# Two transformer layers on one core: running the first attention group inside the neighbouring stages, repeating score matmuls, and keeping the MLP partial sums in SBUF

## The chip, the cores and the metric

The kernel runs on one core of one Trainium2 chip. The metric is the device time of a whole execution in microseconds (us). Executions of the same kernel spread by about 1% here (before: 1991 to 2008 us in its first four runs), so small differences are judged by ratios from interleaved rounds on one chip, with a 95% interval.

The engines are called by their profile names: PE (matmul), PEld (weight load), ACT (activation), DVE (vector), POOL, SP. *Clock* is always the granted TensorE clock of the profile, as a share of full speed. In the profile lines, `S` is a score tile, `P` its exponentials, `tp` a score chunk that DVE copied out, `misc` a PSUM tile of the fill work, `ustg` a staging buffer, `uacc` the partial sums in DRAM and `y` the second MLP product. *PV* is the product of the exponentials with V.

## The reference

```python
x = A_x                                    # 1 x 2048 x 640, bf16
x = x + attention(layernorm(x), wqkv, wo)  # 32 heads of 20
x = x + token_mlp(layernorm(x), w1, b1, w2, b2)   # mixes the 2048 tokens, 1536 hidden, tanh-gelu
x = x + attention(layernorm(x), wqkv, wo)  # same weights again
x = x + token_mlp(layernorm(x), w1, b1, w2, b2)
```

The attention has 4 query blocks of 512, 8 groups of 4 heads and 16 key tiles of 128. One *chunk* is the 128 x 512 score block of one head and one key tile. A layer has 2048 chunks, and each needs an exponential of all its elements.

## The kernel before

A layer of attention is one loop over score tiles of three chunks. PE makes the scores of tile t+1, ACT turns tile t into exponentials, DVE takes one chunk in some of the tiles (five instructions on DVE that build the exponential from bits), and PE multiplies by V. What else PE has to do (projections, output projection, first MLP product) waits in a *fill queue* and is put into the gaps that a small cost model sees.

```python
emit_S(0, 1)
for t in range(NTILES):
    cur_t[0] = t
    if t + 1 < NTILES:
        emit_S(t + 1, 1)            # scores: 3 matmuls of 32 x 128 rows, computed once
    pv_ready(force_t=t - CFG["PT_BUFS"])
    ...
    emit_exp(t)                     # ACT: 3 chunks, or 2 while DVE takes one
    dve_run(clk["act"] - 0.4)
    pv_ready()
    emit_fills(clk["act"], misc_alloc)
```

The token MLP sums over tokens, so its first product can begin with the first query blocks. Before, each of query blocks 0 to 2 makes a partial sum of four token tiles. Every partial sum is copied by DVE into one of two staging buffers, and POOL sends it to DRAM. The second and third partial sums are added there by accumulating DMAs.

```python
ustg = p1.enter_context(tc.tile_pool(name=f"ustg{layer}", bufs=2))
...
def evac(t, ft=ft, c0=c0, c1=c1, w=w):
    stg = ustg.tile([128, 512], F32, name="ustg")
    dve_cost(0.1 + w / 960.0)
    nc.vector.tensor_copy(out=stg[:, 0:w], in_=t[:, 0:w])
    dst = uacc_l[ft * 128:(ft + 1) * 128, c0:c1]
    if p == 0:
        nc.gpsimd.dma_start(out=dst, in_=stg[:, 0:w])
    else:
        nc.gpsimd.dma_start(out=dst, in_=stg[:, 0:w], accum_op=ALU.add)
```

Around the attentions lie four other stages: a prologue (load, LayerNorm, transposes, V, first K and Q), a tail with the first MLP product, a middle stage (second MLP product of layer 0 fused with LayerNorm, transposes, V, first K and Q of layer 1), and at the end the second MLP product of layer 1. No exponential runs in these.

The softmax here doesn't subtract the row's maximum and nothing guards it: scores larger than these inputs give would overflow.

## Time and profile before

1998.11 us median of 4 runs; the profiled execution has a span of 1997.3 us. I cut it into stages with the first and last exponential of each layer and the first matmul that writes `y` (the second MLP product), all read from the timeline:

| stage | from | to | us | bound by |
|---|---|---|---|---|
| prologue | 0 | 49.1 | 49.1 | input DMA, then PE |
| attention 0 | 49.1 | 921.1 | 872.1 | ACT |
| tail and first MLP product | 921.1 | 949.7 | 28.5 | a serial chain, then PE |
| middle | 949.7 | 1039.3 | 89.6 | PE |
| attention 1 | 1039.3 | 1910.2 | 870.9 | ACT |
| tail and first MLP product | 1910.2 | 1939.0 | 28.8 | as above |
| last product | 1939.0 | 1997.3 | 58.3 | PE |

Part 2 of the page, in 40 slices of about 50 us. A digit is the busy share in tenths; PEclk is the granted TensorE clock in tenths.

```profile
PE   7888888889888988878998888888888888888879
ACT  5999999999999998996449999999999999999952
POOL 2000000110012001110000000001100220011000
PEclk9999999996989587886999999999779885888679
```

ACT is at 9 through both attentions, and the clock falls in the second half of each. The costliest ACT groups by shape (columns: line, engine, operation, tiles and shapes, count; busy us, mean ns; idle just before, and who ended it):

```profile
L440 ACT ACTIVATE P<-S 128x1536 bf16<-128x1536 f32 x954 | 1319.0, 1507 | 40.3 <-PE S L351 35.8
L440 ACT ACTIVATE P<-S 128x1024 bf16<-128x1024 f32 x412 | 420.5, 1094 | 22.3 <-PE S L351 21.2 <-ACT P L440 0.3
```

So the exponentials lose 57 us waiting for scores. Windows inside and outside attention (columns: busy us and count of PE, PEld, DVE, ACT, POOL; then clock, DMA share, GB/s):

```profile
660.00:680.00 20.00, 19.02 (x98) 4.29 (x95) 13.02 (x22) 19.78 (x17) 0.00 (x0) 0.50 0.00 1
980.00:1000.00 20.00, 19.89 (x157) 11.85 (x158) 11.28 (x32) 6.96 (x11) 1.64 (x3) 1.00 0.60 193
```

The first is attention at half clock: PE looks 95% busy because every matmul is stretched. The second is the middle stage, where PE is full at full clock.

### The profile page before, as it was taken

Reading aid. Unit: us, or ns where it says so; the run is one execution under the profiler, and the core shown is the slowest. Engines: PE = TensorE matmul, PEld = TensorE weight load, DVE = VectorE, ACT = ScalarE, POOL = GpSimd, SP = SyncE. Lnnn points to the kernel's source line nnn. Section 1 sums busy time; section 2 is a strip of 40 time slices with the busy share of each in tenths; the row PEclk is TensorE's granted clock in tenths of the full one; section 3 lists DMA queues with packets and bytes.
Section 4 is the critical chain, followed back from the end, with each engine's and each line's share of the span. In section 5 each row is a group of like instructions: output and inputs, shape, how many; then the busy total and the mean of one; then the engine's idle time right before and its main releaser. Section 6 shows DMA issues by size and latency. Waiting matters only on the chain.

```text
span 1997.3 us, 29161 instructions
## 1 busy us (share of the span) xinstructions
PE 1700.8 (85%) x11192; PEld 574.9 (29%) x11360; DVE 1490.1 (75%) x2575; ACT 1773.0 (89%) x1504; POOL 150.7 (8%) x218
## 2 busy tenths in 40 slices
PE   7888888889888988878998888888888888888879
PEld 4222222222222222223542222222222222222235
DVE  6887778878777787776567778788778786777662
ACT  5999999999999998996449999999999999999952
POOL 2000000110012001110000000001100220011000
PEclk9999999996989587886999999999779885888679
DMA  5000000120125002324620000012101340132155
GB/s 136 1 1 1 1 1 29 57 75 1 44 44 75 13 30 42 49 28 134 211 93 1 1 1 1 1 42 76 56 1 57 65 68 1 53 51 44 14 155 183
DMA packets 90732, 96.71 MB, mean 48 GB/s; under 512 B 9696, under 2 KB 68192, under 8 KB 90592
## 3 DMA queue, kind: packets, MB, share of 16 engines
q1 hardware_dynamic: 70464, 71.22, 11.4%
q0 software_dynamic: 20128, 23.62, 7.6%
q8 instruction: 89, 1.46, 0.3%
q14 instruction: 51, 0.42, 0.1%
HBM read 55.48 MB, written 39.32 MB: 47 GB/s over the span
## 4 chain that ended last, share of the span: by engine, by line
ACT 35%; issue 27%; PE 26%; DVE 7%; POOL 3%; DMA 2%; SPq 0%; POOLq 0%; ACTq 0%; another core or an unknown queue 0%; DVEq 0%
ACT P L440 34%; PE S L351 7%; PE acc L677 6%; PE y L911 5%; PE misc L230 3%; POOL uacc L559 2%; PE pp L221 1%; DVE tp L450 1%; DMA uacc<-ustg 1%; DVE T L467 1%; PE misc L575 1%; PE big L840 1%; PE misc L547 1%; DVE QTq L638 1%; DMA ua<-uacc 1%
## 5 line engine op out<-in xcount | busy, mean ns | idle before, releaser
L440 ACT ACTIVATE P<-S 128x1536 bf16<-128x1536 f32 (+1 forms) x1366 | 1681.4, 1383 | 62.7 <-PE S L351 57.0
L351 PE MATMUL S<-QTq,KT 32*128 32x512 bf16 x4096 | 602.3, 428 | 229.1 <-ACT P L440 134.7
L677 PE MATMUL acc<-P,Vaug 128*32 128x512 bf16 x3686 | 605.8, 436 | 5.6 <-DVE T L467 5.0
L351 PEld LDWEIGHTS <-KT 32*128 32x128 bf16 x4096 | 194.6, 92 | 666.2 <-issue 467.7
L450 DVE TENSOR_SCALAR tp<-S 128x512 f32<-128x512 f32 x410 | 266.5, 679 | 36.3 <-PE S L351 35.6
L677 PEld LDWEIGHTS <-Vaug 128*32 128x32 bf16 x4096 | 149.2, 95 | 383.3 <-issue 380.7
L413 DVE SCALAR_TENSOR_TENSOR PD<-tp,q 128x1024 int16<-128x1024 f32 (+1 forms) x214 | 252.1, 1178 | 5.8
L403 DVE TENSOR_TENSOR q<-s 128x1024 f16<-128x1024 f16 (+1 forms) x214 | 143.1, 669 | 6.7
L410 DVE TENSOR_TENSOR q<-q,s 128x1024 f16<-128x1024 f16 (+1 forms) x214 | 142.2, 664 | 3.6
L399 DVE TENSOR_SCALAR s<-tp 128x1024 f16<-128x1024 int16 (+1 forms) x214 | 140.2, 655 | 0.1
L467 DVE STREAM_TRANSPOSE T<-acc 128x512 f32<-128x512 f32 x64 | 45.8, 716 | 126.4 <-PE acc L677 126.4
L172 POOL TENSOR_TENSOR rstd<-veps,mhalf 128x1 f32<-128x1 f32 x64 | 36.8, 575 | 1338.5 <-DVE veps L167 924.0
L554 DVE COPY ustg<-misc 128x512 f32<-128x512 f32 (+1 forms) x144 | 70.2, 488 | 84.3 <-PE misc L547 53.8
L547 PE MATMUL misc<-h2st,w1st 128*128 128x128 bf16 (+1 forms) x538 | 120.3, 309 | 9.7 <-DVE ustg L554 4.2
L911 PE MATMUL y<-uT,w2s 128*128 128x128 bf16 (+1 forms) x754 | 106.8, 297 | 4.2 <-ACT uT L854 3.1
L559 POOL DMA_DIRECT2D uacc<-ustg x96 | 84.2, 892 | 310.8 <-DVE ustg L554 292.6
L677 PE MATMUL acc<-PD,Vaug 128*32 128x512 bf16 x410 | 105.7, 433 | 1.7 <-DVE PD L413 1.4
L230 PE MATMUL misc<-hh,wq_pad 128*128 128x512 bf16 x274 | 92.1, 395 | 4.2 <-issue 4.2
L406 DVE TENSOR_SCALAR s<-s 128x1024 f16<-128x1024 f16 (+1 forms) x214 | 88.3, 413 | 5.0
L230 PE MATMUL misc<-hh,wk_pad 128*128 128x512 bf16 x248 | 79.7, 384 | 2.9 <-issue 2.5
L575 PE MATMUL misc<-wo_pad,attnT 128*128 128x128 bf16 (+1 forms) x361 | 76.9, 310 | 0.5 <-issue 0.3
L911 PEld LDWEIGHTS <-w2s 128*128 128x128 bf16 x768 | 59.6, 98 | 50.2 <-issue 5.4
(83 smaller groups left out, 869.8 us busy)
## 6 DMA issues: line engine op xcount, KB each, us to landing
uacc<-ustg POOLq DMA_DIRECT2D x72, 256.0 KB, 3.8
w2s<-in_B_w_dram SPq DMA_DIRECT2D x16, 768.0 KB
w1st<-in_B_w_dram SPq DMA_DIRECT2D x36, 256.0 KB
x1in<-xd SPq DMA_DIRECT2D x24, 320.0 KB
ua<-uacc SPq DMA_DIRECT2D x24, 320.0 KB
xd<-x2s SPq DMA_DIRECT2D x16, 320.0 KB
xin<-xd SPq DMA_DIRECT2D x16, 320.0 KB
uacc<-ustg POOLq DMA_DIRECT2D x72, 64.0 KB, 2.7
```

Source lines behind the costliest of these rows:

```text
L230: pe(nc.tensor.matmul(t[:, :], lhsT=wpad[:, dt_, g, :], rhs=st.hT[:, dt_, tb * 512:(tb + 1) * 512], start=(dt_ == 0), stop=(dt_ == NDT - 1)))
L351: pe(nc.tensor.matmul(St[:, slot, :], lhsT=KT[32 * j:32 * j + 32, g, kt * 128:(kt + 1) * 128], rhs=get_QT(st, qb)[32 * j:32 * j + 32, g, : ...
L399: nc.vector.tensor_scalar(out=s16[:, 0:n_], in0=lo, scalar1=2.0 ** -16, scalar2=0.5 - EXP_S0, op0=ALU.mult, op1=ALU.add)
L403: nc.vector.tensor_tensor(out=q16[:, 0:n_], in0=s16[:, 0:n_], in1=s16[:, 0:n_], op=ALU.mult)
L410: nc.vector.tensor_tensor(out=q16[:, 0:n_], in0=q16[:, 0:n_], in1=s16[:, 0:n_], op=ALU.mult)
L413: nc.vector.scalar_tensor_tensor(out=PD[:, 0:nb, :].rearrange("p a b -> p (a b)").bitcast(I16), in0=tp[:, 0:nb, :].rearrange("p a b -> p ( ...
L440: ex = nc.scalar.activation(out=P[:, 0:na, :].rearrange("p a b -> p (a b)"), in_=St[:, 0:na, :].rearrange("p a b -> p (a b)"), func=ACT.Ex ...
L450: cp = nc.vector.tensor_scalar(out=batch["tp"][:, i, :], in0=St[:, 2, :], scalar1=SCALE * LOG2E * 128.0, scalar2=EXP_MAGIC, op0=ALU.mult, ...
L547: pe(nc.tensor.matmul(t[:, 0:w], lhsT=states[fp]["w"][:, sti, ftl * 128:(ftl + 1) * 128], rhs=tiles4[sti][:, c0:c1], start=(sti == 0), sto ...
L559: nc.gpsimd.dma_start(out=dst, in_=stg[:, 0:w], accum_op=ALU.add)
L677: pe(nc.tensor.matmul(acc[32 * j:32 * j + 32, :], lhsT=Vaug[:, (kt * H + hh) * VW:(kt * H + hh) * VW + 32], rhs=rhs, start=(cnt[j] == 0), ...
L911: pe(nc.tensor.matmul(y[:, 0:w], lhsT=w2s[:, ft, sl * 128:(sl + 1) * 128], rhs=uT[:, ft, c0:c1], start=(ft == 0), stop=(ft == NF - 1)))
```

## The change

The intent is to shorten the ACT-bound stages and to keep ACT fed in them:

1. **Overlap.** The first group of each attention (64 chunks, as 32 tiles of two chunks) runs in the prologue and in the middle stage.
2. **Repeats.** If the fill queue is empty, the scores of a tile are computed twice, to keep PE active.
3. **Sums in SBUF.** The first MLP product starts when query blocks 0 to 2 are done and accumulates all 12 token tiles in PSUM. Its results stay in SBUF, in memory of K, Q and attention tiles that are free by then.
4. **Fixed order.** ACT and POOL are now ordered by the cost model too, not only DVE; a list scheduler orders the prologue and the middle. The normalisation writes 20 instead of 32 columns a head, and V matmuls go in bursts of 3, not 4.

The diff rewrites most of the kernel. Its core, with cuts:

```diff
+    TS = list(range(0, UCH, 2)) + list(range(UCH, len(chunks), 3)) + [len(chunks)]
+    FRONT_TILES = UCH // 2                       # UCH = 64 chunks, one group
...
-                    if t + 1 < NTILES:
-                        emit_S(t + 1, 1)
+            if self.s_next == self.e_next + 1 and self.tile_ready(self.s_next):
+                self.emit_S(1 if (self.fills or self.cur is not None or not fills) else 2)
...
-    PV_BURST=4,
+    PV_BURST=3,
...
-                                    nc.gpsimd.dma_start(out=dst, in_=stg[:, 0:w], accum_op=ALU.add)
+                        nc.vector.tensor_copy(out=home(tr)[:, fl, 0:512], in_=t[:, :])   # SBUF home
...
+                open_psum(pss, "mid", y=1, S=2, misc=1)       # middle stage: before y 3, tp 2, pj 3 buffers
+                run_front(nxt, tasks, dict(y=1, misc=1))      # list scheduler, steps attention in between
...
+            while pending or att.e_next < FRONT_TILES:
```

The instruction orders of both kernels give the counts: 5434 score matmuls against 4096, 3684 chunks on ACT against 3686 and 412 on DVE against 410, and none of the 144 POOL DMAs.

## The prediction

> **What bounds the kernel now.** The windows view splits the 1997 us: prologue until the first exponential at 49 us; attention 0 until 921; tail and first MLP product until 950; second MLP product fused with layer 1's LayerNorm, transposes, V and first K/Q until 1039; attention 1 until 1909; tail and first product until 1939; last product until 1997. In both attentions (1742 us) ACT is the bound: 1366 exponential instructions keep it busy 1681 us (groups by line); in 10 us windows inside attention it idles 61 us. Windows above 0.95 granted clock lose 0.13 us each (111 windows, 15 us), the others 0.78 us each (60 windows, 47 us). Clock 0.50 (460-480, 660-700, 900-920) comes when PE's fill queue is empty, or just after. The Trainium skill (TensorE: Matmul & The Clock Gate, "What's actually happening") says low PE activity halves the clock; the trace agrees, although PE shows as 95% busy there with stretched matmuls. In the middle stage PE is the bound (19.9 of 20 us busy at clock 1.00).
>
> **What the change does** (instruction orders):
> 1. The first group of each attention (64 chunks, 32 two-chunk exponentials) moves into the prologue and the middle stage. At about 0.07 us plus 0.43 us a chunk, fitted to issue intervals, 29.5 us of ACT work per layer leave the ACT-bound stage. Exponentials in all stay the same: 3684 ACT chunks against 3686.
> 2. 1338 repeated score matmuls (5434 against 4096) run when the fill queue is empty, to keep the clock up.
> 3. MLP partial sums stay in SBUF: 144 POOL DMAs, 24 reloads and 144 evictions (70 us of DVE) go; 32 larger evictions come.
> 4. ACT, DVE and POOL follow a fixed order from a cost model.
>
> **On the critical path.**
> - Prologue: PE has about 37 us of work, held back at first by input DMA (share about 1 until 20 us). With scores, PV, tile switches and K/Q of group 1 it is 50 us, starting at 12: end near 65. 49+29.5-65 = 13 us gained.
> - Middle: PE-bound, 89 us from the first y. Scores 7, PV 3.5, switches 10, group-1 projections 2 and stalls behind single y and misc buffers make about 111. 8 us gained: most of the moved work is paid on PE.
> - Attention: warm clock and no DRAM accumulation remove 39 of 61 us idle; some stays, because MLP fills of the last query block wait for K tiles to come free, and a gated queue suppresses the repeats.
> - Tails and first products: a serial LayerNorm chain of 13 us, then 15 us of matmuls; 0 to 2 us gained. Last product: PE-bound, unchanged.
>
> 1998-13-8-39-2 = 1936; I say 1932.
>
> **Predicted: 1932 us, range 1898 to 1966.** Faster by over 2%: 0.82; within 2%: 0.15; slower by over 2%: 0.03.
>
> **What would show it.** First three-chunk exponential near 65 us; attention stages 815 to 830 us each; mean clock above 0.93 without long 0.50 stretches; ACT idle in attention under 30 us in all; middle stage (first y to first three-chunk exponential) 105 to 118 us, PE near 95% busy; exponential busy time still about 1680 us.
>
> **What would make it wrong.** If two passes do not reach the activity threshold, the clock stays low and 25 to 35 us of gain is missing. If the fixed order misjudges DMA arrival, engines block in the prologue (end at 75 or more). If single y and misc buffers serialise the middle, it reaches 125 us and overlap loses there. If stages overlap better than the PE sum says, 1900.

## More of the kernel before

The view of the staging tile says who waits around it (first the two idle lines, then the DMA's time to landing as min/median/max):

```profile
L554 DVE COPY ustg<-misc x144: 251/492/694, 375.6 to 1853.1; 128x512 f32<-128x512 f32 x72, 128x128 f32<-128x128 f32 x72
...
  PE misc L547: 53.8, 73
  DMA uacc<-ustg: 26.6, 14
...
DMA to landing us min/median/max: 1.8/3.2/5.1
```

DVE stood still 26.6 us in 14 waits for a staging buffer whose DMA had not landed.

What such a wait does is in the timeline (start, length, engine, work, idle before and its releaser):

```profile
618.42 0.69 DVE L554 COPY ustg<-misc 128x512 f32<-128x512 f32 x1 [1.84 <-DMA uacc<-ustg]
619.03 1.28 DVE L450 TENSOR_SCALAR tp<-S 128x512 f32<-128x512 f32 x2
...
619.77 0.39 PE L351 MATMUL S<-QTq,KT 32*128 32x512 bf16 x3 [3.10 <-DVE tp L450]
...
620.27 1.45 ACT L440 ACTIVATE P<-S 128x1536 bf16<-128x1536 f32 x1 [2.46 <-PE S L351]
```

Read it downwards. DVE waits 1.84 us for the DMA; behind it in DVE's order stand the two evictions of score chunks; PE can't overwrite that score tile and waits 3.10 us; ACT waits 2.46 us. The engine named as releaser of ACT is PE, but the cause is a DMA two engines away.

Stage lengths are read from one profile a kernel, and they scatter. So a difference of a few us in one attention stage shows nothing by itself.

## The result, and the profile after

The changed kernel takes 1941.1 us median (10 runs, 1929.8 to 1946.4); before is 1995.4 us over 15 runs. The ratio is 0.9711 (interval 0.9687 to 0.9736). Ratios here are the mean time of one kernel's fast runs over that of the other's of the same rounds, so they are not quite the ratio of the medians quoted.

| stage | before us | after us | difference |
|---|---|---|---|
| prologue (after: with group 0 of layer 0) | 49.1 | 75.5 | +26.4 |
| attention 0 (after: without group 0) | 872.1 | 809.6 | -62.5 |
| tail and first product | 28.5 | 33.5 | +5.0 |
| middle (after: with group 0 of layer 1) | 89.6 | 122.8 | +33.2 |
| attention 1 (after: without group 0) | 870.9 | 809.4 | -61.5 |
| tail and first product | 28.8 | 31.9 | +3.1 |
| last product | 58.3 | 57.1 | -1.2 |
| span | 1997.3 | 1939.8 | -57.5 |

The moved group is worth 29.5 us of ACT in each layer (an estimate: 32 x 0.067 + 64 x 0.427 us, which with the counts of before gives 1665 us, against 1681 us measured). The two attentions lost 124 us, 59 of it moved. The two stages that took it in grew by 59.6 us. **So the overlap as built paid back everything it moved, and the whole gain is in attention: 124 - 59 = 65 us, less 8 us that the tails lost.**

The lines of the page after:

```profile
PE   7888888878877789888998888887788777898888
ACT  7899999999999999995157999999999999999942
POOL 5000000000010000000210000000000000000000
PEclk9899999999999999998997999999999999999989
```

The clock stays at 9, and POOL is nearly idle in attention. ACT by shape:

```profile
L484 ACT ACTIVATE P<-S 128x1536 bf16<-128x1536 f32 x910 | 1271.7, 1565 | 9.2 <-PE S L412 8.7
L484 ACT ACTIVATE P<-S 128x1024 bf16<-128x1024 f32 x476 | 492.0, 1127 | 17.7 <-PE S L412 16.6 <-ACT KT L850 0.5
```

Waits for scores fell from 57.0 to 25.3 us, and a little over half of the rest (14 us) is in the overlapped stages. The prologue shows why the overlap costs so much there. First ACT (timeline), then PE in the same time:

```profile
63.68 0.59 ACT L850 CAST KT<-misc 128x512 bf16<-128x512 f32 x1 [0.81 <-PE misc L325]
64.76 0.59 ACT L850 CAST KT<-misc 128x512 bf16<-128x512 f32 x1 [0.49 <-PE misc L325]
65.84 0.59 ACT L850 CAST KT<-misc 128x512 bf16<-128x512 f32 x1 [0.49 <-PE misc L325]
67.30 7.44 ACT L484 ACTIVATE P<-S 128x1024 bf16<-128x1024 f32 x8 [0.88 <-PE S L412]
```

```profile
62.40 4.48 PE L325 MATMUL misc<-hh,wk_pad 128*128 128x512 bf16 x20
66.81 0.39 PE L412 MATMUL S<-QTq,KT 32*128 32x512 bf16 x4
```

The K projections of the *next* group stand in front of the last eight exponentials. The middle stage as one window, before and then after (same columns as above):

```profile
949.65:1039.27 89.62, 84.53 (x645) 49.22 (x655) 51.04 (x142) 30.95 (x46) 8.76 (x16) 1.00 0.51 166
```

```profile
918.63:1041.46 122.83, 111.92 (x774) 56.15 (x789) 55.03 (x120) 48.87 (x67) 18.32 (x32) 0.92 0.42 131
```

PE work rose by 27 us and the idle time of PE from 5 to 11 us; in the last 21 us, from 1020 on, the clock is 0.58, so part of the 27 us is not more work but slower matmuls.

### The profile page after: what moved, and what is told of

Read it like the earlier page. It is cut to its first block, busy times and chain, and to the rows that moved or that the text cites. A ratio compares the mean times of both kernels' runs of the same rounds, so it can differ in the third digit from the quotient of the medians.

```text
span 1939.8 us, 31193 instructions
## 1 busy us (share of the span) xinstructions
PE 1636.4 (84%) x12548; PEld 573.6 (30%) x12698; DVE 1444.4 (74%) x2421; ACT 1750.2 (90%) x1516; POOL 72.9 (4%) x114
## 5 line engine op out<-in xcount | busy, mean ns | idle before, releaser
L484 ACT ACTIVATE P<-S 128x1536 bf16<-128x1536 f32 (+1 forms) x1388 | 1667.6, 1413 | 26.9 <-PE S L412 25.3
L412 PE MATMUL S<-QTq,KT 32*128 32x512 bf16 x5434 | 642.8, 383 | 239.1 <-ACT P L484 180.8
L514 PE MATMUL acc<-P,Vaug 128*32 128x512 bf16 x3684 | 541.7, 392 | 7.7 <-DVE T L572 7.5
L412 PEld LDWEIGHTS <-KT 32*128 32x128 bf16 x5434 | 217.7, 91 | 664.7 <-issue 515.8
L514 PEld LDWEIGHTS <-Vaug 128*32 128x32 bf16 x4096 | 126.5, 93 | 350.1 <-issue 344.8
L998 PE MATMUL y<-uT,w2s 128*128 128x512 bf16 (+1 forms) x747 | 109.7, 297 | 7.2 <-DVE x2s L1004 4.1
L514 PE MATMUL acc<-PD,Vaug 128*32 128x512 bf16 x412 | 86.8, 391 | 8.7 <-DVE PD L461 6.8
L164 DVE CAST QTq<-misc 128x512 bf16<-128x512 f32 x60 | 41.2, 686 | 36.7 <-PE misc L325 34.1
L164 DVE CAST KT<-misc 128x512 bf16<-128x512 f32 x51 | 35.0, 687 | 28.3 <-PE misc L325 17.9
L347 PE MATMUL misc<-wv,hh 128*128 128x500 bf16 (+1 forms) x320 | 54.9, 313 | 0.8 <-DVE Vaug L850 0.8
```

What stands on the lines that cost most here:

```text
L164: nc.vector.tensor_copy(out=out_ap, in_=in_ap)
L412: pe(nc.tensor.matmul(St[:, i, :], lhsT=KT[32 * j:32 * j + 32, g, kt * 128:(kt + 1) * 128], rhs=self.get_QT(qb)[32 * j:32 * j + 32, g, :], ...
L484: ex = nc.scalar.activation(out=P[:, 0:na, :].rearrange("p a b -> p (a b)"), in_=St[:, 0:na, :].rearrange("p a b -> p (a b)"), func=ACT.Ex ...
L514: pe(nc.tensor.matmul(self.acc[32 * j:32 * j + 32, :], lhsT=Vaug[:, (kt * H + h) * VW:(kt * H + h) * VW + 32], rhs=rhs, start=(cnt[j] == 0 ...
L998: pe(nc.tensor.matmul(t[:, c0:c1], lhsT=w2t[sp][:, ft, sl * 128:(sl + 1) * 128], rhs=uT[:, ft, c0:c1], start=(ft == 0), stop=(ft == NF - 1)))
```

## The experiments

Three questions were open. What makes the 65 us in attention: the clock (repeats), the DRAM round trip of the sums, or the new order? Is the overlap worth anything? And what holds the prologue, middle and tails back? All runs gave correct results except one. Ratios are to before, in the same rounds.

### Repeats alone, on the kernel before

```diff
-                        emit_S(t + 1, 1)
+                        emit_S(t + 1, 1 if (fill_queue or fill_state["cur"] is not None) else 2)
```

> The kernel before, with one part of the change alone: every score tile is computed twice when the fill queue is empty (4856 score matmuls instead of 4096). Theory (the low granted clock delays the scores, and the repeats keep the clock up): long stretches of clock 0.50 with an empty queue vanish, mean clock goes from 0.89 to above 0.93, ACT idle in the attention stages falls from 61 us by 15 to 30, total 1965 to 1985 us. Rival (the gain in attention comes from the SBUF sums that replace the accumulating DMAs and evictions, and the clock is a by-product): total within 5 us of before.

Measured: 1985.25 us, just above the expected range, ratio 0.9913 (0.9860 to 0.9966, or 7 to 28 us). The mean clock is 0.965 in the profile (0.946 to 0.954 in the other runs) instead of 0.888. One run of four, the profiled one, took 1969 us and the others 1984 to 1988, so its profile flatters it; ACT's idle time in the attentions is 36 us there instead of 61. The edit also moves the model's choice for DVE a little: DVE takes 404 chunks instead of 410, which costs ACT some 2.6 us (an estimate, 6 x 0.43). The clock row of its page:

```profile
PEclk9999999999999999898999999998999988998989
```

The clock is repaired nearly in full, as the theory says, but the total gains only some 17 us, so most of the 57 us must come from elsewhere.

### The changed kernel without repeats

```diff
-                self.emit_S(1 if (self.fills or self.cur is not None or not fills) else 2)
+                self.emit_S(1)
```

> The changed kernel with the repeated scores taken away (4096 score matmuls instead of 5434), all else the same. Theory (clock): stretches of clock 0.50 come back where the fill queue is empty, mean clock falls to 0.85 or less, attention stages grow from 810 us by 10 to 25 us each, total 1960 to 1990 us. Rival (SBUF sums make the gain): the clock falls but the total stays within 8 us of 1940, since ACT has slack behind a low clock once the other fills are gone.

Measured: 1958.41 us, ratio 0.9798 (0.9752 to 0.9844), mean clock 0.856. That is at the lower edge of the theory (1960 us) and far from the rival (within 8 us of 1940). Attention stages take 821.3 and 818.5 us (809.6 and 809.4 with repeats). Again about 17 us for the repeats. A window at half clock:

```profile
640.00:660.00 20.00, 19.23 (x99) 3.79 (x95) 14.28 (x21) 19.78 (x17) 0.00 (x0) 0.50 0.00 0
```

This kernel has a *lower* mean clock than before (0.856 against 0.888), and still its attention stages, with the 29.5 us added back, are about 22 us shorter each. That is what decides. ACT is busy 19.78 of 20 us at clock 0.50, but so it is in the window of the kernel before shown above, so the line alone shows only that half clock can leave ACT fed. My reading "idle time sits where the clock is low" was a correlation: in 10 us windows of before, those at a clock up to 0.95 lost 0.78 us each; in this kernel they lose 0.29 us (65 windows, 18.5 us). Low clock does not cost the same everywhere; that it costs something, the 17 us of the repeats show.

### One more staging buffer, on the kernel before

```diff
-            ustg = p1.enter_context(tc.tile_pool(name=f"ustg{layer}", bufs=2))
+            ustg = p1.enter_context(tc.tile_pool(name=f"ustg{layer}", bufs=3))
```

> The kernel before, with three staging buffers instead of two for the partial sums on their way to DRAM (the most that fits). Theory (the repeats explain only about 17 of the 57 us; much of the rest is the accumulating DMAs, through DVE waiting 26.6 us for a staging buffer and holding up the score evictions behind it): that wait falls below 12 us, ACT idle in attention falls by 5 to 15 us, total 3 to 12 us shorter than before. Rival (the staging wait is hidden): wait gone, total unchanged within 2 us.

Measured: 1976.99 us against 2005.0 in the same rounds, ratio 0.9848 (0.9806 to 0.9890): more than expected (3 to 12 us). The clock is 0.891, as before the change, and ACT, DVE and POOL run the same instructions in the same order as before, so hardly anything but the wait differs. The staging view now has no line for the DMA at all:

```profile
L554 DVE COPY ustg<-misc x144: 251/472/693, 373.3 to 1832.4; 128x512 f32<-128x512 f32 x72, 128x128 f32<-128x128 f32 x72
...
  PE misc L547: 61.5, 82
```

ACT's waits for scores, from its list of waits (us in total, times, longest), are before and then here:

```profile
ACT P L440 <- PE S L351: 57.0, 107, 2.5
```

```profile
ACT P L440 <- PE S L351: 38.1, 77, 1.0
```

The attentions are 10 and 12 us shorter (862.3 and 858.6 us), ACT's idle time in them 43 us instead of 61. One buffer buys half of what the whole rewrite gains.

### The sums not evicted at all (wrong)

```diff
                             def evac(t, ft=ft, c0=c0, c1=c1, w=w):
+                                if p > 0:
+                                    return
                                 stg = ustg.tile([128, 512], F32, name="ustg")
```

> The kernel before, with a wrong result on purpose: the second and third partial sums are computed on PE but neither evicted nor accumulated in DRAM (96 evictions of 144 and all accumulating DMAs gone; DVE takes 10 more exponential chunks, worth 4 us). Theory (the DRAM round trip of the sums costs most of what the repeats do not explain): attention stages 15 to 22 us shorter each, total 1960 to 1975 us with the clock still low (mean below 0.90). Rival (the rest comes from the fixed order and the burst size, not from the sums): total above 1985 us.

Measured: 1968.09 us, ratio 0.9792 (0.9733 to 0.9850), clock 0.885; attentions 861.6 and 855.7 us. That is within the expected total, but attention 0 is 10.5 us shorter where 15 to 22 were expected. (The profile is of one of the two slower runs, 1975 and 1977 us; the others took 1960 and 1961.) The total is hardly better than with the third buffer (0.9848, intervals overlap), and part of it is the ten chunks that DVE takes over (4 us). So most of what the round trip cost was the *wait for a buffer*; whether the evictions and the accumulation cost some us more is not resolved.

### Both small edits together, on the kernel before

The edit is the two diffs above, repeats and third buffer.

> The kernel before with two small edits together: three staging buffers and the repeated scores. Theory (the two waits are separate, so their gains add: 1.5% and 0.9%): ratio 0.972 to 0.980 to before, 1945 to 1960 us, ACT idle in attention under 25 us, and so most of what the whole rewrite gains, 2.9%. Rival (they cut the same wait: when DVE stalls on staging, the low clock hurts): ratio above 0.982.

Measured: 1951.97 us against 2007.5, ratio 0.9739 (0.9695 to 0.9783). The gains add. ACT idle in the attention windows falls from 61 us to 19 us (12 us in the changed kernel), and the waits for scores to

```profile
ACT P L440 <- PE S L351: 15.0, 38, 1.2
```

Attention takes 848.0 and 844.3 us. Two edited lines give 2.6% where the rewrite gives 2.9%, with overlapping intervals.

A burst of three on top, one rival for the 14 us that still separate these two attentions from the changed kernel's:

```diff
-    PV_BURST=4,
+    PV_BURST=3,
```

> The kernel before with three staging buffers, the repeated scores and, new, bursts of three PV chunks instead of four, as the change sets them. Its attention stages without the burst take 848 and 844 us, the changed kernel's 839 each with the moved 29.5 us added back; 14 us in all are unexplained. Theory (burst size is not the cause; the rest is spread over 96 fewer evictions, the shorter normalisation and the fixed ACT order): ratio to before 0.970 to 0.978, as the run without the burst (0.974). Rival (burst size is most of it): ratio below 0.970, attention stages 842 us or less.

Measured: 1959.63 us against 2006.7, ratio 0.9780 (0.9731 to 0.9829), attentions 851.1 and 845.9 us. The burst shows no gain. What the 14 us are made of stays open; fewer evictions, the shorter normalisation and the fixed ACT order were not separated, and 7 us an attention is no more than the scatter of single profiles (837.7 against 830.2).

### No overlap

```diff
-    TS = list(range(0, UCH, 2)) + list(range(UCH, len(chunks), 3)) + [len(chunks)]
+    TS = list(range(0, len(chunks), 3)) + [len(chunks)]
-    FRONT_TILES = UCH // 2
+    FRONT_TILES = 0
```

> The changed kernel without its overlap: no score, exponential or PV of group 0 runs in the prologue or the middle stage, every score tile has three chunks, all else (buffers, order model, repeats, SBUF sums) stays. Theory (the 59 us of exponentials moved out of attention were paid back in the prologue and the middle stage, so overlap itself is worth about nothing): attention stages about 835 us each, prologue ends near 58, middle near 98, total 1935 to 1955 us, within 1% of the changed kernel. Rival (overlap is worth the 21 us of the prediction): total 1960 us or more.

Measured: 1945.54 us, ratio 0.9729 (0.9692 to 0.9766); the changed kernel has 0.9711. Overlap is worth nothing measurable, as the theory says. The stages of the two profiles show how (gain of overlap, with 29.5 us credited per layer):

| | without overlap us | with overlap us | gain us |
|---|---|---|---|
| prologue | 60.5 + 29.5 | 75.5 | 14.5 |
| middle | 104.1 + 29.5 | 122.8 | 10.8 |
| attention 0 and 1 | 833.3, 834.0 | 809.6 + 29.5, 809.4 + 29.5 | -10.7 |
| both tails | 27.0, 27.0 | 33.5, 31.9 | -11.4 |

Where there is overlap, it does hide 25 us. It gives 11 us back in attention, 7 of them probably because DVE takes no chunk in two-chunk tiles (429 chunks without overlap against 412; 17 x 0.43 = 7 us, an estimate), and 11 us in the tails.

### No overlap, and the freed PSUM given to buffers

Two score tiles take PSUM that the middle stage otherwise has for itself. On top of the edit above:

```diff
-                open_psum(pss, "mid", y=1, S=2, misc=1)
+                open_psum(pss, "mid", y=2, misc=3)
-                run_front(nxt, tasks, dict(y=1, misc=1))
+                run_front(nxt, tasks, dict(y=2, misc=3))
-            open_psum(pss, "pro", S=2, misc=3)
+            open_psum(pss, "pro", misc=5)
-            run_front(att, tasks, dict(misc=3))
+            run_front(att, tasks, dict(misc=5))
```

> As the run without overlap, and the PSUM banks that overlap no longer needs go to deeper buffers: two y tiles and three misc tiles in the middle stage, five misc tiles in the prologue. Theory: the single y and misc buffers make the middle stage wait, so it falls to 86 to 92 us as before the change, and the total to 1928 to 1942 us, as fast as the changed kernel or a little faster. Rival (the middle stage is bound by PE work alone): middle and total as in the run without overlap, within 3 us.

Measured: 1929.2 us, ratio 0.9654 (0.9613 to 0.9695). That is clear of the run without overlap in the same rounds (1940 to 1947 us against 1928 to 1936) and better than the changed kernel (0.9711), though the intervals of these two just touch. The prologue ends at 56.9 instead of 60.5 us. The middle stage as one window, without overlap and then with deep buffers too:

```profile
920.84:1024.92 104.08, 90.66 (x665) 50.72 (x665) 49.45 (x110) 24.24 (x45) 18.37 (x32) 1.00 0.49 154
```

```profile
917.61:1007.75 90.14, 87.08 (x665) 50.17 (x665) 52.75 (x123) 18.68 (x31) 18.00 (x32) 1.00 0.49 160
```

The same 665 matmuls at the same clock; PE idles 13.4 us with single buffers and 3.1 us with deep ones. With single buffers the waits of PE in this window begin with these two, for a `y` and a `misc` tile to be copied out; with deep ones neither is in the list:

```profile
PE y L998 <- DVE x2s L1004: 3.8, 5, 1.0
PE misc L347 <- ACT Vaug L850: 2.7, 4, 0.7
```

The PSUM that overlap needs costs 14 us of a middle stage without overlap. With 29.5 us credited the deep buffers come to 119.6 us, the overlap to 122.8.

### Overlap only in the prologue

The list of tiles becomes one per layer: two-chunk tiles and overlap in layer 0, none in layer 1, with the deep middle buffers.

```diff
-    TS = list(range(0, UCH, 2)) + list(range(UCH, len(chunks), 3)) + [len(chunks)]
-    FRONT_TILES = UCH // 2
+    TSL = (list(range(0, UCH, 2)) + list(range(UCH, len(chunks), 3)) + [len(chunks)],
+           list(range(0, len(chunks), 3)) + [len(chunks)])
+    FTL = (UCH // 2, 0)
```

> Overlap in the prologue only; in layer 1 no overlap and deep buffers in the middle stage (two y tiles, three misc tiles). Theory (from stage lengths: the prologue with overlap does 29.5 us of exponentials and ends at 75.5, against 57 to 60 without; the middle with overlap takes 123 against 90): prologue overlap gains about 11 us over none, less 4 us for exponential chunks that DVE can't take there, so total 1920 to 1929 us, 0 to 10 us below the kernel without any overlap. Rival (prologue overlap is worth nothing either): 1930 us or more.

Measured: 1926.38 us, ratio 0.9627 (0.9599 to 0.9655). The total falls in the theory's range, but the step from no overlap with deep buffers (0.9654) is inside the noise. Against the changed kernel the intervals don't overlap.

### Three attempts at the prologue and the tail

In the prologue one LayerNorm apply on DVE took ten times its usual 0.44 us, at the same time as a POOL memset (DVE timeline, then POOL timeline, of the changed kernel):

```profile
44.29 4.34 DVE L879 TENSOR_SCALAR h_bf<-x0in,mv,rstd 128x640 bf16<-128x640 bf16 x1
```

```profile
44.09 4.36 POOL L148 MEMSET wo_pad<- 128x5120 bf16 x1
```

The edit moves this memset to ACT at the start:

```diff
-        nc.gpsimd.memset(wo_pad[:], 0.0)
...
+            nc.scalar.memzero(wo_pad[:])
```

> The changed kernel with the zeroing of the padded output weights moved from POOL (4.36 us inside the prologue) to ACT's idle time near 6 us. Theory (the one LayerNorm apply on DVE that took 4.34 us instead of 0.44 was locked out by that POOL memset, and everything behind it on DVE slipped): no apply above 0.6 us, prologue overlap ends 2 to 4 us earlier, near 72 instead of 75.5. Rival (the slow apply waited for something else, or is off the chain): the end stays at 75 to 76.

Measured, one look: the apply takes 0.44 us, so the lock-out by the memset is shown:

```profile
44.30 0.44 DVE L878 TENSOR_SCALAR h_bf<-x0in,mv,rstd 128x640 bf16<-128x640 bf16 x1
```

But the overlapped prologue ends at 74.7 instead of 75.5 us, where the theory had 72. The mechanism holds and its size is a miss: the apply was hardly on the chain.

The next run adds to the mixed kernel this move and leaves three of four group-1 K projections to the fill queue:

```diff
-            for tb in range(NQB):
+            for tb in range(1):
                 tasks += front_group(att, 1, tb, tuple(pads_rest) + (evT[4 * tb + 3],))
```

> As the mixed kernel, with two edits in the prologue: the padded output weights are zeroed on ACT near 6 us, not by POOL, and three of the four K projections of group 1 leave the prologue for the attention's fill queue. Theory (each lies on the prologue's chain: 4 us of DVE lock-out, 3.3 us of PE before the last exponentials): prologue overlap ends 4 to 8 us earlier, total 4 to 8 us below the mixed kernel. Rival (PE has no slack at the start of attention and pays the projections back): within 3 us of it.

Measured: 1926.75 us, ratio 0.9627, the same as the mixed kernel. The overlapped prologue did end 4.3 us earlier (71.4 against 75.7), and attention 0 ended at 884.0 us in both. The outcome is the rival's: attention paid it all back. That it did so because PE has no slack there was not tested.

The last run packs the fills of the final query block so that no partial-sum matmul is left behind the attention:

```diff
-                self.emit_fills(clk["act"])
+                self.emit_fills(clk["act"] + (0.05 if self.unit >= (NQB - 1) * NG * NKT else 0.0))
```

> The mixed kernel (overlap in the prologue only, deep buffers in the middle), with the zeroing of the output weights on ACT and with 0.05 us more room in the model's budget for fills in the last query block, so that no matmul of the partial sums is left after the last score tile (42 to 50 were left before). Theory (the leftovers delay the first MLP product behind each attention: 33 us of tail in layer 0 against 27): tail 0 falls to 27 us or less, total 1915 to 1924 us. Rival (the fills packed tighter delay the scores and attention pays it back): total within 3 us of the mixed kernel at 1926.

Measured: 1925.25 us, ratio 0.9600 (0.9567 to 0.9633), not clear of the mixed kernel, as the rival had it. Tail 0 falls from 33.3 to 30.0 us (27 expected), but tail 1 grows from 27.0 to 29.1. PE in tail 1 of the mixed kernel (some leftovers, and then the first product, here named `S<-hh,KT` after the buffers that it reuses), and then in tail 0 of this kernel (none):

```profile
1848.14 0.89 PE L722 MATMUL misc<-hh,wv 128*128 128x128 bf16 x8
1848.87 0.71 PE L954 MATMUL S<-hh,KT 128*128 128x512 bf16 x4
1850.98 12.72 PE L954 MATMUL S<-hh,KT 128*128 128x512 bf16 x90 [1.40 <-ACT hh L196]
```

```profile
895.14 1.22 PE L953 MATMUL S<-hh,KT 128*128 128x512 bf16 x4 [3.28 <-DVE x1last L939]
897.48 15.44 PE L953 MATMUL S<-hh,KT 128*128 128x512 bf16 x92 [1.11 <-ACT hh L195]
```

Without leftovers PE idles while DVE and ACT do the last LayerNorm, and the product then starts at clock 0.62 (window 897.5 to 905) where the other runs at 1.00 (window 1851 to 1858). The same tail 1 of this last kernel, now without leftovers, agrees: clock 0.68 from 1851 to 1858, and 15.0 us for the product instead of 12.7. So in these kernels a few leftovers cost nothing and keep the clock up, while the many of tail 0 delay the product.

## Why the prediction was right or wrong, point by point

The total was right: 1932 forecast with 1898 to 1966, 1941 measured. The sum behind it was not, and that the total came out is in good part luck.

- **"Attention: warm clock and no DRAM accumulation remove 39 of 61 us idle."** The direction was right and the size too small: 65 us went, and the windows show 12 us of idle left of 61. The exponentials' busy time also fell, from 1681 to 1668 us. A likely reason, not tested, is that they overlap where ACT does not wait: by their means, those of before would take 1888 us one after another (954 x 1.507 + 412 x 1.094) and took 1681. I weighed the causes wrongly. I tied the idle time to the clock, because it sat in windows of low clock. The repeats are worth some 17 us (in both directions, before with them and after without them); the staging buffer alone gives 1.5%. The step that failed is reading a cause from where the idle time lies, instead of following single waits back through DVE to the DMA.
- **"49+29.5-65 = 13 us gained" in the prologue.** It ended at 75.5, so 3 us. I named 75 as the failure mark and gave late DMA arrival as its cause. No run tested that; DVE waited for input only 2.1 us. What the runs show is that the new prologue takes 60.5 us instead of 49.1 even without overlap (56.9 with deeper buffers; the rest of this growth stays open), and that K projections of the next group hold up the last exponentials. Shortening it by 4.3 us brought nothing, because attention 0 then took as much longer.
- **"Middle ... 8 us gained".** It takes 122.8 us, not 111: a loss of 4. The parts named come to 111.5 without any stall (89 + 7 + 3.5 + 10 + 2), so the stalls behind single y and misc buffers were named and counted as nothing. Measured, the stage grew by 33 us instead of 22.5: PE idles 6 us more than before (10.9 against 5.1; waits for a free y tile make 4.1 us of the 10.9), and its busy time rose by 27 us, with the clock at 0.58 in the last 21 us, which the sum did not have. The length of the failure case (125 us) was nearly reached, but its cause, single buffers, is only a part.
- **"Tails and first products ... 0 to 2 us gained".** They lost 8. Partial-sum matmuls were left over after the attention; I had not looked for them in the instruction order, where they stand. They are part of the loss: without them tail 0 still took 30.0 us.
- **Last product unchanged:** right (57.1 against 58.3). **Exponential work unchanged:** right in counts. **Mean clock above 0.93:** right (0.98).

The three misses on overlap (10, 12 and 9 us) and the miss on attention (26 us) nearly cancelled.

## What to carry to other kernels

When the bound engine waits for another one, follow a few single waits to their end before naming a cause: here a DMA landing reached ACT through a staging buffer, DVE's order and a score tile, and one more buffer did half the work of a rewrite. Work moved from a full stage into a neighbour was not gained here, and can only be if that neighbour has slack in the engine *and* in the memory it needs; credit the stages in pairs, and test "the same kernel without the overlap, with its memory given to buffers". A profile slice where two things coincide (low clock and idle) needs a run that changes only one of them.

## What the Trainium skill lacked or had wrong

- *TensorE: Matmul & The Clock Gate*, "What's actually happening": it says the gate follows how busy PE has been recently. The runs agree (clock 0.50 in attention with an empty fill queue, near 1.00 with repeated scores), but the page gives no share of activity at which the gate opens, and the profile's busy share doesn't tell: PE showed 19.02 us busy of 20 at clock 0.50. A low clock is not yet lost time: ACT stayed 19.78 of 20 us busy in that window, while over the whole kernel the repeats that lift the clock gained some 17 us.
- *SBUF — State Buffer*, "Who interferes with whom": it says a DVE `tensor_scalar` in a 2-port mode is blocked for the whole of a POOL instruction that came first. The trace agrees: 4.34 us instead of 0.44 beside a 4.36 us memset, and 0.44 again without it. (That the apply ran in such a mode, no run shows.) So nothing is wrong here; the prologue ended 0.8 us earlier in the one run that moved the memset.
- *DMA: Bandwidth & Descriptors*, "Anatomy of one DMA": its fit for POOL-issued DMAs (2.0 us plus bytes over 436 GB/s) gives 2.6 us for 256 KB. The 72 transfers of 256 KB in the trace of before have a median of 3.8 us from issue to landing, but they are of two kinds. The 24 plain ones have a median of 2.5 us, so the fit holds; the 48 accumulating ones have 3.9 us. The page gives no figure for accumulating DMAs, nor for their longer issue on POOL (0.86 us median against 0.54 for plain ones).
